# Strassen blocks for the first FFN's input products, float64 weights decoded by ACT's parametric ReLU, and split weights kept in DRAM, in a kernel of attention and two FFNs

## The chip, the cores and the metric

The kernel runs on one core of one Trainium2 chip. The metric is the device time of one execution in microseconds. Engines: PE multiplies matrices (PEld is its weight load), DVE works elementwise on vectors, ACT evaluates functions and copies, POOL is a third elementwise engine which here also can issue DMAs, and SP issues DMAs. SBUF is the on-chip memory, PSUM holds the eight banks that PE accumulates into.

## What is computed

```python
def reference(q, k, v, moe_w_gate, moe_w_val, moe_w_out, moe_rms_g, moe2_w_in, moe2_w_out):
    x = causal_attention(q, k, v)            # (2, 12, 448, 64) -> (896, 768), float32
    xn = x / sqrt(mean(x * x) + 1e-6) * moe_rms_g
    g = xn @ moe_w_gate                      # 768 -> 1536
    y = (g * sigmoid(g) * (xn @ moe_w_val)) @ moe_w_out          # 1536 -> 768
    h = y @ moe2_w_in                        # 768 -> 2048
    return maximum(0.01 * h, h) @ moe2_w_out                     # 2048 -> 768
```

All weights of the FFNs arrive as float64 (8 bytes a number, read on the chip as pairs of 32-bit words: `top` and, in the changed kernel, `low`).

## The kernel before

There are two batches of 448 tokens (b = 0, 1), 768 features in six blocks of 128, and feature-major tiles of 128 x 448. Each float32 operand is kept as a high and a low part of PE's fp32r type, and each product of two 128-blocks is three matmuls into one PSUM bank: high x high, high x low, low x high (lines 657 to 659, 879 to 881 and 1006 to 1008).

*Weights.* A float64 weight tile (128 x 768, 768 KB) is loaded by SP into one of two `raw` tiles, turned into float32 in `x` by one ACT scaling (line 308, or 263 in the second FFN) and three DVE instructions: a 16-bit copy (310, 265), a shift with a mask (312, 267) and a shift with an or (315, 270). Then it is split into high and low: ACT copies the high part (317, or 283 by halves), DVE subtracts for the low part (319, 284). `weight` does this for the first FFN into four `hl` tiles; `convert` and `split` do it by halves for the second.

*First FFN.* A column tile `fc` (12 of them, 128 columns each) of gate and value needs 6 blocks x 3 matmuls for each of g, v and each batch. `gate` issues these 18, `gate_out` applies silu, multiplies and splits the result into a `big` tile. Tiles 0 to 4 are done early for batch 0, beside the attention of batch 1; tiles 3 and 4 for batch 1 follow with the weights that are still there; tiles 5 to 11 are done for both batches; then the weights of tiles 0 to 2 are loaded, decoded and split a second time for batch 1. The output product runs over six column tiles `dc` with all 12 blocks in one go in two banks. When a `dc` is done, its y is split and four sums and differences of batch halves are formed and split (lines 809 to 828).

*Second FFN.* `pair` does two column tiles of the input product for both batches by one level of Strassen's method in Winograd's form: 2 x 2 blocks (columns by feature halves times feature halves by batches), seven block products of 3 x 3 matmuls in place of eight. Weight sums and differences are formed on DVE (888 to 923), banks are passed on by ACT copies (939, 943) and DVE additions (946, 949). `partial` multiplies a chunk of four results with the output weights and adds to partial sums in SBUF: ACT copies the partial sum into the bank (997) and back out (1015). The order is pair 0, pair 1, chunk 0, pair 2, pair 3, chunk 1, and so on.

*What sets the order.* Every step is registered with `add(engine, cost, ..., rank)`. `Order.emit` goes through the steps with those costs and fixes, for each engine, one static order: of the steps that are ready, the one of lowest rank goes first. A table `ADJUST` shifts single ranks of attention and early weights. On the chip each engine works through its own list strictly, waiting on semaphores; SP issues loads, the small transfers of the attention (`mrow`, `st`) and the outputs from one list.

Of the kernel before, what the change touches and what calls it, by code (L numbers as in the profile page):

```python
# [8 lines left out]
F32 = mybir.dt.float32  # L9
# [4 lines left out]
U16 = mybir.dt.uint16  # L14
# [8 lines left out]
    ("cut", 0): 19, ("cut", 1): 9, ("cut", 2): 7, ("cut", 3): 12, ("cut", 4): 43, ("cut", 6): 5,  # L23
    ("cut", 8): 21, ("cut", 10): 9, ("cut", 11): 18, ("exp", 0): 10, ("exp", 1): 59, ("exp", 2): 4,
    ("exp", 3): -11, ("exp", 4): -13, ("exp", 5): 39, ("exp", 7): 33, ("exp", 8): 83, ("exp", 9): 57,
    ("exp", 10): -21, ("g", 0, 0): -36, ("g", 2, 0): -51, ("g", 3, 0): -10, ("g", 4, 0): 49, ("gw", 0): -7,
    ("gw", 1): 35, ("gw", 2): 41, ("gw", 4): 11, ("gw", 5): 28, ("inv", 0): 253, ("inv", 1): 45,
    ("inv", 2): 28, ("inv", 3): -1, ("inv", 5): -49, ("inv", 8): -16, ("inv", 9): 30, ("inv", 10): -32,
    ("inv", 11): 54, ("max", 0): -4, ("max", 1): -68, ("max", 2): -70, ("max", 3): -16, ("max", 4): 14,
    ("max", 5): -17, ("max", 6): -33, ("max", 7): -38, ("max", 8): -5, ("max", 9): -8, ("max", 10): 36,  # L30
    ("max", 11): -2, ("mul", 1): 4, ("mul", 3): -23, ("mul", 5): -15, ("mul", 7): 9, ("mul", 9): -14,
    ("mul", 10): 21, ("round", 0): -22, ("round", 4): 42, ("round", 6): 51, ("round", 7): 11,
    ("round", 8): -50, ("round", 9): 119, ("round", 10): -8, ("row", 0): -43, ("row", 2): 6, ("row", 3): 24,
    ("row", 4): 5, ("row", 5): -100, ("row", 7): -18, ("row", 8): -6, ("row", 9): -13, ("row", 10): -178,
    ("sq", 0): -30, ("sq", 2): 3, ("sq", 3): -9, ("sq", 4): 34, ("sq", 5): -38, ("sq", 7): -22, ("sq", 8): -9,
    ("sq", 9): 8, ("sq", 11): -1, ("sum", 0): 49, ("sum", 1): 149, ("sum", 2): 1, ("sum", 3): 28,
    ("sum", 5): -19, ("sum", 6): 60, ("sum", 7): -70, ("sum", 8): -21, ("sum", 9): -51, ("sum", 10): 28,
    ("sum", 11): 10, ("turn", 0): -30, ("turn", 1): -8, ("turn", 2): 1, ("turn", 3): 8, ("turn", 5): 21,
    ("turn", 6): 46, ("turn", 7): -155, ("turn", 8): -9, ("turn", 9): -10, ("turn", 10): -44,
    ("turn", 11): 25, ("v", 1, 0): -14, ("v", 3, 0): -97, ("v", 4, 0): -96, ("val", 0): -90, ("val", 1): -183,  # L40
    ("val", 3): -120, ("val", 4): 50, ("val", 5): -22, ("val", 6): -21, ("val", 7): 3, ("val", 8): 13,
    ("val", 9): -43, ("val", 10): 17, ("val", 11): 13, ("vw", 0): -38, ("vw", 1): 189, ("vw", 3): -6,
    ("vw", 4): -94, ("vw", 5): -20,
}

# [98 lines left out]
def causal_attention_two_ffns(  # L144
# [61 lines left out]
    y = xn  # L206
# [3 lines left out]
    NT1 = B * KF  # L210
    NBIG = NT1 + 6
# [3 lines left out]
    tmps, parts = [], []  # L215
    tctx = ExitStack()
    order = [(fc, 0) for fc in range(EARLY)]
    order += [(fc, b) for fc in range(KF) for b in range(B) if (fc, b) not in order]
    t_slot = {k: n for n, k in enumerate(order)}
    NG = 12  # L220
    g_slot = {(fc, b): HK + (fc * B + b) % NG for fc in range(KF2) for b in range(B)}

    queue = []
    for fc in list(range(KF)) + list(range(EARLY - 2)):
        again = len(queue) >= 2 * KF
        queue += [(("g", fc, again), w_gate[fc]), (("v", fc, again), w_val[fc])]
    out_order = [dc for k in range(HK) for dc in (k, k + HK)]  # L230
# [11 lines left out]
    halves2 = [(hl, j) for hl in range(NHL) for j in range(2)]  # L242
    half_turn = [0]

    def convert(key, rank):

        n = slot[key]
        src = queue[n][1]
        raw, t = raws[n % NRAW], n % NX2
        kr, kx = ("raw", n % NRAW), [("x", t, 0), ("x", t, 1)]  # L250
        top = raw.bitcast(U32).rearrange("p (n t) -> p n t", t=2)[:, :, 1]
        halves = raw.bitcast(U16).rearrange("p (n t) -> p n t", t=4)
# [5 lines left out]
        def half(j):  # L258
            return lambda: xs32[t][:, j * HK * P:(j + 1) * HK * P]

        add("SP", 0.35, lambda: nc.sync.dma_start(out=raw, in_=src), r=[("split", n - NRAW)], w=[kr],
            rank=rank - 30, name=(key[0] + "d", key[1], 0), late=2.0, size=1024 * NW)
        add("ACT", 0.9, lambda: nc.scalar.activation(xs32[t], top.bitcast(F32), AF.Copy, scale=2.0 ** -112),  # L263
            r=[kr], w=kx + ([("x", t)] if t < NX else []), rank=rank, name=name)
        add("DVE", 0.56, lambda: nc.vector.tensor_copy(halves[:, :, 2], halves[:, :, 1]), port=True,  # L265
            w=[kr], rank=rank, name=name)
        add("DVE", 0.56, port=True, name=name, fn=lambda: nc.vector.tensor_scalar(
            top.bitcast(I32), top.bitcast(I32), 13, -0x7FFFFFF9, ALU.arith_shift_right, ALU.bitwise_and),
# [822 lines left out]
```

## Time and profile before

| what | value |
|---|---|
| time, median of 3 runs (lowest to highest) | 606.61 us (605.12 to 611.77) |
| profiled execution | 608.25 us |
| its span from first to last instruction | 606.5 us |
| PE busy | 590.6 us, 97% |
| DVE busy | 454.9 us, 75% |
| ACT busy | 319.3 us, 53% |
| DMA | 70.38 MB, mean 116 GB/s |
| chain of work that ended last | PE 85%, DVE 7%, DMA 3%, ACT 2%, issue 2% |

Matmuls overlap: one takes some 366 ns from its start to its end, but starts follow each other at about 0.2 us, so busy time merges overlapping matmuls, and the number that counts is the distance between starts. A view by stretches gives, for each stretch of time, the busy time of each engine with the number of instructions in brackets, the granted clock of PE as a share of full speed, and the DMA share.

### The profile page before, as it was taken

The numbers are of one execution on the slowest core, as the hardware profiler recorded it, in microseconds if no ns is written. First come the engines' busy times: TensorE is split into PE (matmuls) and PEld (weight loads), VectorE is DVE, ScalarE is ACT, GpSimd is POOL, SyncE is SP. The second block draws the span as 40 slices with busy tenths as digits, with TensorE's granted clock in tenths as the row PEclk, the third lists the DMA queues.
The fourth block names the chain that finished last, engine by engine and source line by source line (L and its number), as shares of the span: only waits on it lengthen the run. The fifth ranks groups of instructions, "written<-read, shape, count | busy, mean of one in ns | idle before, by whom it ended". The sixth has DMA issues, their size and how long they took to land.

```text
span 606.5 us, 8664 instructions
## 1 busy us (share of the span) xinstructions
PE 590.6 (97%) x3224; PEld 503.9 (83%) x3224; DVE 454.9 (75%) x844; ACT 319.3 (53%) x553; POOL 54.5 (9%) x84
## 2 busy tenths in 40 slices
PE   8989799999999999999999999899999999999997
PEld 6544456588999999999999999789999999999996
DVE  6678798789897666668778672997898879878920
ACT  3556675846444333344335331665587658746841
POOL 1246445430000000000000000000000000000000
PEclk8989899999999999999999999999999999999999
DMA  5283840443444333234444231205423342333122
GB/s 191 68 184 99 204 103 3 107 106 108 154 156 157 104 105 105 104 109 161 153 156 150 105 111 45 101 5 160 163 94 116 145 156 69 139 105 105 52 92 91
DMA packets 18714, 70.38 MB, mean 116 GB/s; under 512 B 6000, under 2 KB 7536, under 8 KB 18672
## 3 DMA queue, kind: packets, MB, share of 16 engines
q1 hardware_dynamic: 18672, 69.83, 36.5%
q8 instruction: 25, 0.41, 0.3%
q14 instruction: 17, 0.14, 0.1%
HBM read 66.85 MB, written 2.75 MB: 115 GB/s over the span
## 4 chain that ended last, share of the span: by engine, by line
PE 85%; DVE 7%; DMA 3%; ACT 2%; issue 2%; SPq 1%; POOL 0%; DVEq 0%; ACTq 0%
PE bank L657 13%; PE bank L659 13%; PE bank L658 13%; PE bank L1008 7%; PE bank L1007 7%; PE bank L1006 7%; PE bank L879 5%; PE bank L881 5%; PE bank L880 5%; PE bank L485 3%; PE bank L527 2%; PE bank L421 2%; PE bank L539 1%; DMA mrow<-mt 1%; PE bank L479 1%
## 5 line engine op out<-in xcount | busy, mean ns | idle before, releaser
L657 PE MATMUL bank<-xn,hl 128*128 128x448 f32 x288 | 106.7, 370 | 0.3 <-ACT sg L700 0.3
L659 PE MATMUL bank<-xn,hl 128*128 128x448 f32 x288 | 105.5, 366 | 0.1
L658 PE MATMUL bank<-xn,hl 128*128 128x448 f32 x288 | 105.2, 365 | 0.0
L1006 PE MATMUL bank<-big,hl 128*128 128x448 f32 x192 | 70.7, 368 | 0.0
L1007 PE MATMUL bank<-big,hl 128*128 128x448 f32 x192 | 70.7, 368 | 0.0
L1008 PE MATMUL bank<-big,hl 128*128 128x448 f32 x192 | 70.7, 368 | 0.0
L657 PEld LDWEIGHTS bank<-xn,hl 128*128 128x128 f32 x288 | 54.1, 188 | 7.1 <-issue 1.4
L319 DVE TENSOR_TENSOR hl<-x,hl 128x768 fp32r<-128x768 f32 x42 | 39.9, 955 | 25.0 <-ACT hl L317 24.7
L659 PEld LDWEIGHTS bank<-xn,hl 128*128 128x128 f32 x288 | 54.1, 188 | 5.4 <-DVE hl L319 1.1
L429 DVE CUSTOM_DVE_ANT_0 bank<-bank,maskw 112x224 f32<-112x224 f32 (+2 forms) x96 | 42.3, 469 | 20.6 <-PE bank L421 19.8
L658 PEld LDWEIGHTS bank<-xn,hl 128*128 128x128 f32 x288 | 54.1, 188 | 4.1
L317 ACT CAST hl<-x 128x768 fp32r<-128x768 f32 x42 | 34.9, 834 | 40.5 <-DVE x L315 22.9
L658 PE MATMUL bank<-big,hl 128*128 128x448 f32 x144 | 52.6, 365 | 0.0
L657 PE MATMUL bank<-big,hl 128*128 128x448 f32 x144 | 52.6, 365 | 0.0
L659 PE MATMUL bank<-big,hl 128*128 128x448 f32 x144 | 52.6, 365 | 0.0
L284 DVE TENSOR_TENSOR hl<-x,hl 128x384 fp32r<-128x384 f32 x72 | 38.8, 556 | 14.0 <-ACT hl L283 13.9
L310 DVE COPY raw<-raw 128x768 uint16<-128x768 uint16 x42 | 43.9, 1044 | 7.2 <-ACT x L308 7.0
L308 ACT ACTIVATE x<-raw 128x768 f32<-128x768 f32 x42 | 38.2, 909 | 9.2 <-DMA raw<-in_val 2.5
L283 ACT CAST hl<-x 128x384 fp32r<-128x384 f32 x72 | 35.6, 513 | 12.2 <-PE bank L880 4.1
L315 DVE SCALAR_TENSOR_TENSOR x<-x,raw 128x768 uint32<-128x768 uint32 x42 | 40.4, 962 | 0.8
L265 DVE COPY raw<-raw 128x768 uint16<-128x768 uint16 x32 | 33.4, 1043 | 9.6 <-ACT x L263 9.6
L1007 PEld LDWEIGHTS bank<-big,hl 128*128 128x128 f32 x192 | 36.0, 188 | 3.7
(120 smaller groups left out, 1162.8 us busy)
## 6 DMA issues: line engine op xcount, KB each, us to landing
raw<-in_out SPq DMA_DIRECT2D x28, 768.0 KB
raw<-in_in SPq DMA_DIRECT2D x16, 768.0 KB
raw<-in_gate SPq DMA_DIRECT2D x10, 768.0 KB
raw<-in_val SPq DMA_DIRECT2D x10, 768.0 KB
qkv<-in_qkv SPq DMA_DIRECT2D x32, 176.0 KB
raw<-in_gate SPq DMA_DIRECT2D x20, 192.0 KB
raw<-in_val SPq DMA_DIRECT2D x20, 192.0 KB
out<-sg SPq DMA_DIRECT2D x12, 224.0 KB
```

What stands on the lines that cost most here:

```text
L284: add("DVE", 0.5, port=True, name=name, fn=lambda: nc.vector.tensor_tensor(out=t[:, 1], in0=src(), in1=f32(t[:, 0]), op=ALU.subtract), r=[ ...
L308: add("ACT", 0.9, lambda: nc.scalar.activation(x[:, :w], top.bitcast(F32), AF.Copy, scale=2.0 ** -112), r=landed, w=[kx], rank=rank, name= ...
L310: add("DVE", 0.56, lambda: nc.vector.tensor_copy(halves[:, :, 2], halves[:, :, 1]), port=True, w=[kr], rank=rank, name=name)
L315: add("DVE", 0.96, port=True, name=name, fn=lambda: nc.vector.scalar_tensor_tensor(xb, xb, 3, top, ALU.logical_shift_left, ALU.bitwise_or) ...
L319: add("DVE", 0.96, port=True, name=name, fn=lambda: nc.vector.tensor_tensor(out=hl[:, 1, :w], in0=x[:, :w], in1=f32(hl[:, 0, :w]), op=ALU. ...
L429: nc.vector.tensor_tensor_reduce(out=s, in0=s, in1=maskw[:, S - w:S], scale=-1.0, scalar=3.0e38, op0=ALU.add, op1=ALU.min, accum_out=m[:, ...
L657: nc.tensor.matmul(o, hi, xh, start=s, stop=False, skip_group_check=True)
L658: nc.tensor.matmul(o, hi, xl, start=False, stop=False, skip_group_check=True)
L659: nc.tensor.matmul(o, lo, xh, start=False, stop=e, skip_group_check=True)
L1006: nc.tensor.matmul(bank(), hi, xh, start=s, stop=False, skip_group_check=True)
L1007: nc.tensor.matmul(bank(), hi, xl, start=False, stop=False, skip_group_check=True)
L1008: nc.tensor.matmul(bank(), lo, xh, start=False, stop=e, skip_group_check=True)
```

## The change

The changed kernel keeps the arithmetic of the parts but arranges the FFNs as follows.

- Tiles 5 to 11 of the first FFN (gate and value of one `fc` as the two columns) go through `pair`, as the second FFN's do. For this the two batch differences and sums of xn are formed once in `token_sums` from the float32 x, which is now kept in 12 tiles.
- The first FFN's output product is done in four chunks, over tiles (3, 4), (0, 1, 2), (5, 6, 7) and (8 to 11), with partial sums in the x tiles; `chunk` is one function for both FFNs.
- The float64 decoding is one ACT instruction with the parametric ReLU (slope 2^32 on the negative side) and two DVE instructions on the low word; the 16-bit copy is gone.
- The split weights of tiles 0 to 2 are stored to DRAM by SP (six stores of 768 KB) during the attention and reloaded by POOL's queue.
- Whole weight tiles are split at once into six wide tiles (and one half of each pair into two slim ones) in place of halves in four. The leaky ReLU is one ACT instruction. The sums of weights are formed in place.
- The second FFN's order is pairs 0, 1, 2, chunk 0, pairs 3, 4, chunk 1, and so on. Tiles are shared between stages, `ADJUST` has other numbers.

```diff
 ADJUST = {
-    ("cut", 0): 19, ("cut", 1): 9, ("cut", 2): 7, ("cut", 3): 12, ("cut", 4): 43, ("cut", 6): 5,
+    ("cut", 0): -30, ("cut", 1): -51, ("cut", 2): -5, ("cut", 3): 47, ("cut", 4): 7, ("cut", 5): -9,
...
+OUT1_CHUNKS = [3, 4], [0, 1, 2], [5, 6, 7], [8, 9, 10, 11]
+FIRST_FFN = [
+    ("n", 3), ("n", 4), ("n", 0), ("n", 1), ("c", 0), ("n", 2), ("s", 5), ("c", 1), ("s", 6), ("s", 7), ("s", 8),
+    ("c", 2), ("s", 9), ("s", 10), ("s", 11), ("c", 3),
+]
...
-        add("ACT", 0.9, lambda: nc.scalar.activation(xs32[t], top.bitcast(F32), AF.Copy, scale=2.0 ** -112),
...
-        add("DVE", 0.56, lambda: nc.vector.tensor_copy(halves[:, :, 2], halves[:, :, 1]), port=True,
...
+        add("ACT", 0.9, lambda: nc.scalar.activation(xs32[t], top.bitcast(F32), AF.Prelu, scale=2.0 ** -112,
+            alpha=2.0 ** 32),
...
         add("DVE", 0.56, port=True, name=name, fn=lambda: nc.vector.tensor_scalar(
-            top.bitcast(I32), top.bitcast(I32), 13, -0x7FFFFFF9, ALU.arith_shift_right, ALU.bitwise_and),
+            low, low, 29, None, ALU.logical_shift_right), w=[kl], rank=rank)
...
     def weight(key, rank, at=0.0):
+        hl, kh = hls[hl_of(key)], ("hl", hl_of(key))
+        if key in kept:
+            add("POOL", 1.3, lambda: nc.gpsimd.dma_start(out=hl, in_=stored[key[:2]]), r=[("kept", key[:2])], w=[kh],
+                rank=rank - 30, late=2.0, size=1024 * NW)
+            return
...
+        if (*key[:2], True) in kept:
+            add("SP", 0.35, lambda: nc.sync.dma_start(out=f32(stored[key[:2]]), in_=f32(hl)), r=[kh], w=[("kept", key[:2])],
+                rank=rank - 20, late=2.0, size=1024 * NW)
...
+    def pair(key1, key2, rank):
+        wr = rank - 2
+        a1, (a11, a12) = convert(key1, wr)
+        a2, (a21, a22) = convert(key2, wr)
+        A11, A12 = split(a1, wr)
+        A22, = split(a22, wr, False)
+        combine(a21, a11, a21, ALU.subtract, wr)
+        combine(a22, a22, a21, ALU.subtract, wr)
+        S3, S2 = split(a2, wr)
+        combine(a12, a12, a22, ALU.subtract, wr)
+        combine(a11, a22, a11, ALU.add, wr)
+        S1, S4 = split(a1, wr)
...
+    def gated(fc, rank):
+        (g0, kg0), (g1, kg1), (v0, kv0), (v1, kv1) = pair(("g", fc, False), ("v", fc, False), rank)
...
+    def token_sums(k, rank):
+        def both(b, dc, dst):
+            hi_lo(lambda: x32[b * KD + dc], x_key(b, dc), *dst, rank, ["room"])
+        minus((0, k), (1, k), (0, k), rank)
+        both(0, k, of_sum(0, k))
...
```

In the order of the instructions, three places matter. The first is PE's list in the first FFN: gate, then value of a column tile before (`hl_71`, `hl_70` the split weights, `bank_75`, `bank_76` the sums), and the first Strassen pair (tile 5) in the changed kernel.

```order
L658 MATMUL bank_75<-xn,hl_71 128x448
L659 MATMUL bank_75<-xn,hl_71 128x448
L657 MATMUL bank_76<-xn,hl_70 128x448
L658 MATMUL bank_76<-xn,hl_70 128x448
L659 MATMUL bank_76<-xn,hl_70 128x448
```

```order
L889 MATMUL bank_76<-xn,hl_68 128x448
L890 MATMUL bank_76<-xn,hl_68 128x448
L995 MATMUL bank_72<-big_93,hl_71 128x448
L996 MATMUL bank_72<-big_93,hl_71 128x448
L997 MATMUL bank_72<-big_93,hl_71 128x448
L888 MATMUL bank_79<-sum_1500,hl_70 128x448
L889 MATMUL bank_79<-sum_1500,hl_70 128x448
L890 MATMUL bank_79<-sum_1500,hl_70 128x448
L888 MATMUL bank_79<-sum_1501,hl_70 128x448
```

Blocks of nine matmuls on xn and on the token sums have taken the place of runs of 18, and a product of the next chunk (lines 995 to 997) stands between two blocks.

The second is DVE's list where weight tiles are decoded: two tiles of the first FFN's output weights before, and the weights of a pair (tile 6) in the changed kernel.

```order
L310 COPY raw_64<-raw_64 128x768
L312 TENSOR_SCALAR raw_64<-raw_64 128x768
L315 SCALAR_TENSOR_TENSOR x_66<-x_66,raw_64 128x768
L310 COPY raw_65<-raw_65 128x768
L312 TENSOR_SCALAR raw_65<-raw_65 128x768
L319 TENSOR_TENSOR hl_70<-x_66,hl_70 128x768
L315 SCALAR_TENSOR_TENSOR x_67<-x_67,raw_65 128x768
```

```order
L312 TENSOR_TENSOR more_1513<-x_67,more_1513 128x768
L295 SCALAR_TENSOR_TENSOR x_67<-x_67,raw_64 128x768
L897 TENSOR_TENSOR x_67<-x_66,x_67 128x384
L293 TENSOR_SCALAR raw_65<-raw_65 128x768
L295 SCALAR_TENSOR_TENSOR x_1518<-x_1518,raw_65 128x768
L312 TENSOR_TENSOR hl_68<-x_66,hl_68 128x768
L933 TENSOR_TENSOR sg_1517<-bank_77,sg_1516 128x448
```

Each tile has one instruction less for decoding; half-wide sums (line 897) and the pair's recombination (line 933) have come in between.

The third is SP's list in the middle of the attention (`qkv` are the attention's inputs, `mrow` the row maxima, `st` the row sums, `raw` the weights).

```order
L400 DMA qkv_96<-in_qkv 32x1408 x4
L465 DMA mrow_101<-mt_113 4x4x112
L556 DMA st_125<-sm_121 128x1x14 x2
L465 DMA mrow_102<-mt_114 4x4x112
L400 DMA qkv_93<-in_qkv 32x1408 x4
```

```order
L433 DMA qkv_111<-in_qkv 32x1408 x4
L498 DMA mrow_120<-mt_132 4x4x112
L354 DMA stored_g_105<-hl_68 128x1536
L589 DMA st_140<-sm_138 128x1x14 x2
L498 DMA mrow_121<-mt_133 4x4x112
L433 DMA qkv_112<-in_qkv 32x1408 x4
```

A store of 768 KB now stands ahead of small transfers that the attention waits for; there are six such stores in the list, and POOL's list has got six loads at its end.

## Rows read from the trace of the kernel before

**Rows 1.** Part 1 of the page: busy time, share of the span, instructions.
```profile
PE 590.6 (97%) x3224; PEld 503.9 (83%) x3224; DVE 454.9 (75%) x844; ACT 319.3 (53%) x553; POOL 54.5 (9%) x84
```
**Rows 2.** Stretches of 50 us: busy (count) of PE, PEld, DVE, ACT, POOL; clock; DMA.
```profile
0.00:50.00 50.00, 45.42 (x341) 28.23 (x342) 34.23 (x142) 24.31 (x39) 14.28 (x34) 0.90 0.53 148
50.00:100.00 50.00, 45.41 (x385) 26.41 (x379) 42.42 (x132) 32.78 (x59) 24.06 (x34) 0.97 0.47 110
...
150.00:200.00 50.00, 50.00 (x249) 46.33 (x248) 42.88 (x58) 23.11 (x34) 0.00 (x0) 1.00 0.43 144
...
350.00:400.00 50.00, 47.18 (x231) 42.49 (x229) 34.77 (x59) 22.00 (x43) 0.00 (x0) 1.00 0.24 79
400.00:450.00 50.00, 50.00 (x242) 45.44 (x243) 43.95 (x73) 29.60 (x57) 0.00 (x0) 1.00 0.37 126
```
**Rows 3.** PE alone in the two long stretches without idle time: busy (matmuls), clock.
```profile
143.30:379.65 236.35, 236.35 (x1167) 1.00 0.36 122
400.30:602.60 202.30, 202.30 (x980) 1.00 0.32 110
```
**Rows 4.** Timeline of PE from 380 to 400 us: start, us, instruction, idle before.
```profile
381.47 0.47 PE L879 MATMUL bank<-xn,hl 128*128 128x448 f32 x1 [1.44 <-ACT hl L283]
...
392.24 0.47 PE L879 MATMUL bank<-big,hl 128*128 128x448 f32 x1 [0.59 <-DVE sg L946]
...
399.98 0.47 PE L879 MATMUL bank<-xn,hl 128*128 128x448 f32 x1 [0.79 <-ACT bank L943]
```
**Rows 5.** Who PE waited for until 150 us: us in total, times, longest.
```profile
PE bank L479 <- DMA mrow<-mt: 2.8, 2, 1.8
PE bank L421 <- ACT qkr L411: 2.2, 2, 1.5
...
PE bank L421 <- DVE m L429: 1.0, 3, 0.6
PE bank L539 <- DVE mt L463: 0.8, 1, 0.8
PE bank L460 <- DVE mhl L458: 0.7, 2, 0.4
```
**Rows 6.** Groups of instructions by line and shape: count, busy us, mean ns, idle before.
```profile
L310 DVE COPY raw<-raw 128x768 uint16<-128x768 uint16 x42 | 43.9, 1044 | 7.2 <-ACT x L308 7.0
L315 DVE SCALAR_TENSOR_TENSOR x<-x,raw 128x768 uint32<-128x768 uint32 x42 | 40.4, 962 | 0.8
L319 DVE TENSOR_TENSOR hl<-x,hl 128x768 fp32r<-128x768 f32 x42 | 39.9, 955 | 25.0 <-ACT hl L317 24.7
L284 DVE TENSOR_TENSOR hl<-x,hl 128x384 fp32r<-128x384 f32 x72 | 38.8, 556 | 14.0 <-ACT hl L283 13.9
L308 ACT ACTIVATE x<-raw 128x768 f32<-128x768 f32 x42 | 38.2, 909 | 9.2 <-DMA raw<-in_val 2.5 <-DVE hl L319 2.4 <-DMA raw<-in_out 2.0
...
L312 DVE TENSOR_SCALAR raw<-raw 128x768 int32<-128x768 int32 x42 | 25.0, 596 | 1.2
...
L1015 ACT COPY part<-bank 128x448 f32<-128x448 f32 x36 | 19.1, 531 | 24.6 <-PE bank L1008 24.4
...
L946 DVE TENSOR_TENSOR sg<-bank,sg 128x448 f32<-128x448 f32 x8 | 5.0, 620 | 2.1 <-PE bank L881 2.1
...
L559 DVE SCALAR_TENSOR_TENSOR r<-st 128x14 f32<-128x14 f32 x12 | 4.0, 337 | 0.0
```
**Rows 7.** Timeline from 116 to 122 us, SP's queue, POOL and DVE.
```profile
116.77 2.52 SPq L301 DMA_DIRECT2D raw<-in_val  x4
...
118.52 1.44 POOL L582 TENSOR_TENSOR acc<-acc,sq 128x448 f32<-128x448 f32 x1 [0.74 <-ACT sq L579]
...
118.87 1.12 DVE L559 SCALAR_TENSOR_TENSOR r<-st 128x14 f32<-128x14 f32 x1
...
121.17 1.04 DVE L310 COPY raw<-raw 128x768 uint16<-128x768 uint16 x1
```
**Rows 8.** Engines in 10 us after a stall of PE: PE, PEld, DVE, ACT, POOL, clock.
```profile
60.00:70.00 10.00, 8.27 (x65) 4.55 (x65) 7.13 (x24) 5.42 (x10) 3.66 (x6) 0.83 0.90 197
```

More of the change, by code (lines that the diff above doesn't have):

```diff
@@ L33 @@
[L33 to L37, printed above, removed]
@@ L288, in weight, with split, t @@
-    def weight(key, rank, at=0.0):
-        n = slot[key]
-        src = queue[n][1]
+            xb(), xb(), 3, low, ALU.logical_shift_left, ALU.bitwise_or), r=[kl], w=kx + [("split", n)], rank=rank)
+        return (lambda: xs32[t], kx), [(half(j), [kx[j]]) for j in range(2)]
+    def split(part, rank, wide=True):
+        src, keys = part
+        turn, n = (wide_turn, NWIDE) if wide else (slim_turn, NSLIM)
+        m = turn[0] % n
+        turn[0] += 1
+        key = ("hl", m) if wide else ("slim", m)
+        def t(e):
+            return (slims[m] if not wide else hls[m] if m < NHL else more[m - NHL])[:, e]
+        add("ACT", 0.83 if wide else 0.51, lambda: nc.scalar.copy(t(0), src()),
+            r=keys if wide and m < NHL else keys + ["room"], w=[key], rank=rank)
+        add("DVE", 0.96 if wide else 0.56, port=True, fn=lambda: nc.vector.tensor_tensor(
+            out=t(1), in0=src(), in1=f32(t(0)), op=ALU.subtract), r=keys, w=[key], rank=rank)
+        return [(t, key, j) for j in range(2 if wide else 1)]
@@ L865, in of_y, with x_key @@
[L865 to L881 removed]
+    def x_key(b, k):
+        return ("x32", b * KD + k)
@@ new lines, in minus, with of_x, of_sum @@
+    def minus(o, p, q, rank):
+        (bo, ko), (bp, kp), (bq, kq) = o, p, q
+        o, p, q = (x32[b * KD + k] for b, k in (o, p, q))
+        add("DVE", 0.63, port=True, fn=lambda: nc.vector.tensor_tensor(out=o, in0=p, in1=q, op=ALU.subtract),
+            r=[x_key(bp, kp), x_key(bq, kq)], w=[x_key(bo, ko)], rank=rank)
+    def of_x(b, k):
+        return lambda e: xn[:, e, k, b * S:(b + 1) * S], ("xn", b, k)
+    def of_sum(n, k):
+        return lambda e: sums[n * HK + k][:, e], ("sum", n, k)
@@ new lines, in block @@
+    def block(u, weights, xs, first, rank, name):
+        t, wk, j = weights
+        def passes(k, x):
+            hi, lo = (t(e)[:, (j * HK + k) * P:(j * HK + k + 1) * P] for e in range(2))
+            o = banks[u][:, :S]
+            nc.tensor.matmul(o, hi, x(0), start=first and not k, stop=False, skip_group_check=True)
+            nc.tensor.matmul(o, hi, x(1), start=False, stop=False, skip_group_check=True)
+            nc.tensor.matmul(o, lo, x(0), start=False, stop=k == HK - 1, skip_group_check=True)
```

535 lines of the change are left out of this document (239 added, 296 removed).

## The prediction

> **What bounds the kernel now.** I read the page's first part, then the engines by stretches, then PE alone. PE is busy for 590.6 of 606.5 us, DVE for three quarters and ACT for half [rows 1]. By stretches the span has two regimes [rows 2]. From 0 to about 143 us (attention, with early first-FFN tiles beside it) PE has holes: 4.6 us in each of the first two stretches of 50 us. After that PE shows 50.00 of 50 us almost everywhere, and only the stretch at 350 us lacks 2.8 us, so nothing but PE's own work or that hole can be shortened there.
>
> How long that work takes is the distance between matmul starts, which the stretches of PE alone give [rows 3]. Between 143.30 and 379.65 us, 1,167 matmuls follow each other without a hole, which is 1,166 steps: 236.35 / 1,166 = 202.7 ns each. Between 400.30 and 602.60 us it is 202.30 / 979 = 206.6 ns, at the same granted clock of 1.00 and the same tile sizes. So there are two paces, 3.9 ns apart, and the pace changed at a restart, after PE had stood still at 399.98 us [rows 4]; it stayed to the end. The slower pace costs 979 x 3.9 ns = 3.8 us.
>
> The hole between 380 and 400 us is the passage from the first FFN to the second: PE waits 1.44 us for an ACT split of pair weights, 0.59 us for a DVE addition and 0.79 us for an ACT copy, 2.82 us in all [rows 4]. There DVE had to split y and its sums and decode the pair's weights at once.
>
> **The change part by part.** I sum against the profiled execution, 608.25 us (span 606.5 plus 1.75 around it); it lies 1.64 us above the median, 606.61.
>
> *Fewer matmuls.* A first-FFN tile for both batches is 2 x 2 x 6 products of three matmuls, 72. As a pair it is seven blocks of nine, 63. Seven tiles (5 to 11) change, so 7 x 9 = 63 matmuls go, all in the regime in which PE has no holes. At 202.7 ns that is 12.8 us (at 206.6 ns, 13.0). Tiles 0 to 4, the output products and the second FFN keep their counts. Value: -12.8 us.
>
> TensorE's rule would give less. The Trainium skill (TensorE: Matmul & The Clock Gate, Back-to-back issue gap) gives N/2.4 + 2.5 ns for an isolated stream, 189 ns at N = 448, so an estimate of 11.9 us for 63; the trace's 202.7 ns disagrees and is what I use.
>
> *The passage at 380 us.* Decoding a tile before costs DVE 1,044 + 596 + 962 ns, a whole split 955, a half split 556, a sum of 448 columns 620 [rows 6]. A pair before: 2 x 2.60 for decoding, seven half splits and four half sums at 0.556, ten instructions of 0.62 for the results: 17.5 us. A pair now: 2 x 1.56 (the 1,044 ns copy is gone; the shift works on as many words as the old one, so I take its 596 ns), three wide splits, one half split, four half sums, six instructions of 0.62: 3.1 + 2.9 + 2.8 + 3.7 = 12.5 us, against 63 x 0.2027 = 12.8 us of PE. The six wide tiles also let the first pair be ready before y is. So the causes of the 2.82 us shrink, but y's splits and sums still fall due within the last chunk. I take half: -1.4 us; ends -2.8 and 0.
>
> *New work late in the first FFN.* Tiles 9 to 11 and the last chunk take PE 333 x 0.2027 = 67.5 us. In that time DVE must prepare tiles 10 and 11 (2 x 8.8), finish three tiles (3 x 3.7), decode and split four output weights (4 x 2.51), form y's sums (33 x 0.62, of which the last 5 us fall behind the chunk) and prepare the first pair of the second FFN (8.8): about 63 us, 93%. The fullest stretch in which DVE before kept PE without holes is 43.95 of 50 us, 88% [rows 2]. If 88% is all that DVE can do, the 63 us need 71.1, 3.6 us too many; if it can do 93%, nothing is lost. I take +1.0; ends 0 and +3.6. ACT has room: it is busy 53% before [rows 1], and the chunks add 36 copies into and 36 out of banks at 0.53 us [rows 6], 38 us over the 213 us of PE in the first FFN.
>
> *The pace.* Some restarts in the trace lead to the quick pace, the last one to the slow. I can't tell which the changed kernel falls into; I take a little more of the quick one than before, -1.0; ends -3.8 (all quick) and +4.3 (the 1,103 quick ones that remain become slow).
>
> *Attention.* The decoding of ten early tiles loses its copy: 10 x 1.044 = 10.4 us of DVE in a regime where DVE is busy 42.4 of 50 us [rows 2]. PE waits there for DVE for 1.0 + 0.8 + 0.7 = 2.5 us, for `mrow` transfers 2.8 us and for ACT behind a `qkv` load 2.2 us [rows 5]. I take 1.5 us of the DVE waits as gained. The six stores (a tile of 768 KB each, in SP's list ahead of `mrow` and `st`) come on top of ten loads of the same size beside which those 2.8 us of `mrow` waits arose: 0.28 us a transfer, so +1.7 us for six. A stall costs more than itself: in the 10 us with the 1.5 us wait of PE the clock is 0.83 [rows 5, 8]. Sum +0.2; ends -4 (all DVE waits and part of the others go, with their clock) and +6 (1 us a store).
>
> *The reload.* Tile 0's gate weights go into `hl2` when batch 1 of tile 3 has done with them, and PE's list has 18 products, 54 matmuls or 10.9 us, before it wants them. A load of that size took at most 4.4 us from its issue to the first DVE instruction on it [rows 7]. So it is hidden with 6.5 us to spare, as for the others; six decodings and splits go from DVE and ACT, and PE sees nothing: 0. The ACT instruction with the parametric ReLU I take at the 909 ns of the scaling it replaces [rows 6]; it is on no path that PE waits for, and the list of ACT has four table loads before and after.
>
> Sum: -12.8 - 1.4 + 1.0 - 1.0 + 0.2 = -14.0, so 608.25 - 14.0 = 594.2 for an execution like the profiled one, and less 1.64, 592.6 for the median.
>
> **The rivals.**
>
> *DVE becomes the bound* (same within 1%). The first FFN's end at 88% costs 3.6 in place of 1.0, the holes at 380 us stay (0 in place of -1.4), and every restart falls into the slow pace (+4.3 in place of -1.0): 592.6 + 2.6 + 1.4 + 5.3 = 601.9 us. For it: 93% is more than any stretch before. Against: over the whole first FFN from 143 us DVE has about 175 us of work for 213 us of PE, and the second FFN falls from some 88% to 35.0 of 54.7 us for two pairs and a chunk.
>
> *The reload comes late* (about the same). In the trace a small DVE instruction (337 ns on average) took 1.12 us while POOL added two tiles [rows 6, 7]: the two engines hold each other up. If a reload issued by POOL were held up in the same ratio, three times a load, 13.2 us in place of 4.4, each of the first four would miss its 10.9 us by 2.3 us: +9.2, 601.8 us. Against: DVE is not busy without a break there, and the last two reloads have a chunk's time. The Trainium skill (SBUF — State Buffer, SBUF: two separate sides) speaks for this rival: a DMA from POOL's queue has its descriptors written by POOL, which two-port DVE instructions (shifts among them) lock out. No run so far has such a DMA; the skill's example is 0.62 us that became 3.1, which as an estimate adds 2.5 us and stays under the cover.
>
> *The stores choke the attention* (slower). Each of the six stores stands ahead of small transfers for which PE waits within microseconds. If each held PE back by its whole 4.4 us, that is 26.4 us in place of my 1.7: 617.3 us. It decides from (606.6 - 590.9) / 6 = 2.6 us a store. For it: PE did wait 1.8 us for one `mrow` [rows 5]. Against: ten transfers of the same size cost 2.8 us together.
>
> *It doesn't do what it says*: if the planner filled the Strassen blocks with other work, the count would stay. PE's list has 2,928 rows in place of 2,991, exactly 63 fewer, so I give this nothing.
>
> **How the numbers follow.** My forecast has 0.79, with its own range of 585 to 600; DVE as the bound 0.12; the late reload 0.05; the choking stores 0.04. A measurement of this kernel tells about 1% from no change, 600.5 to 612.7 us. Of the forecast nearly all (0.78) lies below 600.5, of the DVE rival 0.05 and of the reload 0.03 when they come in part: faster 0.86. The rest of these is 0.10 for the same, and the stores make 0.04 slower. The low end, 584, has all holes at 380 us gone, the quick pace throughout and half of the best end in the attention (592.6 - 1.4 - 1.0 - 2.8 - 2.1 = 585.3, a microsecond below for spread); the high end, 601, takes in most of the two middle rivals.
>
> **What would show it.** Right: 63 matmuls fewer at 202 to 207 ns; no hole of PE over 1 us between the attention's end and the last matmul; DVE some 70 us less busy in all; reloads landing before PE wants them. Wrong: PE waiting for DVE splits in tiles 9 to 11 or in the last chunk of the first FFN; PE waiting for `mrow` next to a store, with a clock of 0.8 in that slice; PE waiting for a DMA from DRAM near 150 us. The forecast fails if these add to more than about 8 us.

## The result and the profile after

The changed kernel takes 586.54 us, the median of four executions (595.38, 586.67, 586.10, 586.41), against 607.26 for the kernel before (605.12 to 611.77). The ratio is 0.965 with the interval 0.958 to 0.972: 3.5% faster. The forecast was 592.6, 584 to 601: the direction and the range held, and the number was 6 us too high. One thing is needed to read the times: they fall into two groups 9 us apart, near 586 and near 595; the ratio uses the first group, while the profile is of the execution of 595.38 us (span 593.7).

Busy time and instructions on the page, as [rows 1]:

```profile
PE 581.8 (98%) x3161; PEld 492.5 (83%) x3161; DVE 391.7 (66%) x760; ACT 374.5 (63%) x636; POOL 52.2 (9%) x90
```

63 matmuls are gone, DVE is 63.2 us less busy, ACT 55 us more. The stretches of 50 us, as [rows 2], then PE alone in one of 400 us, as [rows 3] (busy time with the count, clock, DMA):

```profile
0.00:50.00 50.00, 45.35 (x329) 27.61 (x331) 34.35 (x136) 24.09 (x39) 12.94 (x35) 0.90 0.52 141
50.00:100.00 50.00, 46.52 (x403) 26.66 (x399) 40.77 (x133) 33.48 (x61) 21.43 (x34) 0.97 0.61 164
150.00:200.00 50.00, 50.00 (x244) 45.41 (x243) 33.06 (x56) 25.81 (x46) 3.41 (x6) 1.00 0.51 174
350.00:400.00 50.00, 50.00 (x244) 45.41 (x243) 43.12 (x70) 35.77 (x61) 0.00 (x0) 1.00 0.29 98
400.00:450.00 50.00, 50.00 (x243) 45.42 (x242) 33.29 (x50) 31.86 (x52) 0.00 (x0) 1.00 0.40 139
```

```profile
150.00:550.00 400.00, 400.00 (x1937) 1.00 0.36 123
```

The hole at 350 us, 2.8 us before, is gone: the whole stretch is 50.00. But PE now starts 244 matmuls in 50 us where before it started 249 in the stretch at 150 us: 400 / 1,936 = 206.6 ns, the slower of the two paces of [rows 3], at the same clock of 1.00, and here from the attention's end to the last matmul. Behind 145 us PE waits for nothing. What it waited for before that, as [rows 5]:

```profile
PE bank L512 <- DMA mrow<-mt: 3.2, 4, 1.6
...
PE bank L454 <- ACT qkr L444: 1.1, 2, 0.8
PE bank L512 <- ACT p L541: 0.9, 2, 0.7
PE bank L454 <- DVE m L462: 0.6, 2, 0.4
PE bank L493 <- DVE mhl L491: 0.6, 2, 0.4
```

Decoding and splitting, as [rows 6], and the reloads (median us from issue to landing at the end):

```profile
L295 DVE SCALAR_TENSOR_TENSOR x<-x,raw 128x768 uint32<-128x768 uint32 x58 | 55.3, 956 | 26.8 <-ACT x L290 25.9
L312 DVE TENSOR_TENSOR hl<-x,hl 128x768 fp32r<-128x768 f32 x48 | 45.5, 955 | 39.8 <-ACT hl L310 39.7
...
L290 ACT ACTIVATE x<-raw 128x768 f32<-128x768 f32 x58 | 52.6, 910 | 1.6 <-DMA raw<-in_gate 0.9
...
L293 DVE TENSOR_SCALAR raw<-raw 128x768 uint32<-128x768 uint32 x58 | 32.2, 557 | 14.0 <-DMA raw<-in_out 10.0
```

```profile
hl<-stored_g POOLq DMA_DIRECT2D x3, 768.0 KB, 4.8
hl<-stored_v POOLq DMA_DIRECT2D x3, 768.0 KB, 4.6
```

The parametric ReLU takes 910 ns, the scaling that it replaced 909. The reloads take 4.8 and 4.6 us in the median and 6.7 at most, of a forecast cover of 10.9.

Where the time went, profile against profile, by the starts in the two traces. The attention's last restart of PE is at 141.58 us with 2,169 matmuls to come; before it was at 143.05 with 2,230, two fewer than 2,169 + 63. So the attention ends 1.47 - 0.4 = 1.1 us earlier. The 63 matmuls are 12.8 us. Behind its restart before took 459.56 us from the first start to the last, 7.8 more than 2,229 steps of 202.7 ns; 3.9 of that is the pace of 979 matmuls, so the three holes cost not 2.8 but 3.9 us with the longer steps around each restart. After takes 448.13 us, 8.7 more than at 202.7 ns, and has no hole: that is the slow pace alone. At the quick one it would gain 1.1 + 12.8 + 3.9 + 3.9 = 21.7 on the profiled execution's 608.25, which makes 586.6: the first group of times. The slow pace for all 2,169, 8.6 us, makes the second. The 586.6 is the measure for the experiments below.

Late in the first FFN, where the prediction saw DVE as nearly full, the 333 matmuls of tiles 9 to 11 and of the last chunk stand between 297.90 and 366.7 us (1,080 follow, all of the second FFN). Columns as above:

```profile
297.90:366.70 68.80, 68.80 (x334) 62.51 (x333) 52.62 (x84) 45.15 (x78) 0.00 (x0) 1.00 0.31 103
```

DVE is busy there for 52.6 us, 76%, and not for 63.

### The profile page after: what moved, and what is told of

Its sections match the earlier page's. It is cut to its first block, busy times and chain, and to the rows that moved or that the text cites. A ratio compares the mean times of both kernels' runs of the same rounds, so it can differ in the third digit from the quotient of the medians.

```text
span 593.7 us, 8477 instructions
## 1 busy us (share of the span) xinstructions
PE 581.8 (98%) x3161; PEld 492.5 (83%) x3161; DVE 391.7 (66%) x760; ACT 374.5 (63%) x636; POOL 52.2 (9%) x90
## 4 chain that ended last, share of the span: by engine, by line
PE 90%; DMA 5%; DVE 2%; SPq 1%; ACT 1%; issue 1%; ACTq 0%; DVEq 0%
PE bank L997 12%; PE bank L996 12%; PE bank L995 12%; PE bank L890 11%; PE bank L888 11%; PE bank L889 11%; PE bank L690 5%; PE bank L691 4%; PE bank L692 4%; PE bank L518 3%; PE bank L560 2%; DMA mrow<-mt 2%; PE bank L454 1%; PE bank L512 1%; DMA st<-sm 1%; DMA raw<-in_gate 1%
## 5 line engine op out<-in xcount | busy, mean ns | idle before, releaser
L295 DVE SCALAR_TENSOR_TENSOR x<-x,raw 128x768 uint32<-128x768 uint32 x58 | 55.3, 956 | 26.8 <-ACT x L290 25.9
L1006 ACT COPY x<-bank 128x448 f32<-128x448 f32 x72 | 38.3, 532 | 51.0 <-PE bank L997 50.8
L995 PE MATMUL bank<-big,hl 128*128 128x448 f32 x147 | 54.1, 368 | 0.0
L996 PE MATMUL bank<-big,hl 128*128 128x448 f32 x147 | 54.1, 368 | 0.0
L997 PE MATMUL bank<-big,hl 128*128 128x448 f32 x147 | 54.1, 368 | 0.0
L290 ACT ACTIVATE x<-raw 128x768 f32<-128x768 f32 x58 | 52.6, 910 | 1.6 <-DMA raw<-in_gate 0.9
L995 PE MATMUL bank<-big,more 128*128 128x448 f32 x135 | 49.7, 368 | 0.0
L996 PE MATMUL bank<-big,more 128*128 128x448 f32 x135 | 49.7, 368 | 0.0
L997 PE MATMUL bank<-big,more 128*128 128x448 f32 x135 | 49.7, 368 | 0.0
L690 PE MATMUL bank<-xn,hl 128*128 128x448 f32 x120 | 45.5, 379 | 0.0
L692 PE MATMUL bank<-xn,hl 128*128 128x448 f32 x120 | 44.1, 367 | 0.0
L691 PE MATMUL bank<-xn,hl 128*128 128x448 f32 x120 | 44.0, 367 | 0.0
L293 DVE TENSOR_SCALAR raw<-raw 128x768 uint32<-128x768 uint32 x58 | 32.2, 557 | 14.0 <-DMA raw<-in_out 10.0
L722 DVE TENSOR_TENSOR big<-sg,big 128x448 fp32r<-128x448 f32 x47 | 28.6, 621 | 18.8 <-ACT big L721 18.8
L888 PE MATMUL bank<-xn,hl 128*128 128x448 f32 x105 | 38.6, 368 | 0.0
L889 PE MATMUL bank<-xn,hl 128*128 128x448 f32 x105 | 38.6, 368 | 0.0
L890 PE MATMUL bank<-xn,hl 128*128 128x448 f32 x105 | 38.6, 368 | 0.0
L987 ACT COPY bank<-x 128x448 f32<-128x448 f32 x72 | 37.9, 536 | 1.2
L541 ACT ACTIVATE p<-bank 128x512 f32<-128x512 f32 x48 | 26.1, 596 | 17.3 <-PE bank L518 17.3
```

The source lines that it names most:

```text
L295: add("DVE", 0.96, port=True, name=name, fn=lambda: nc.vector.scalar_tensor_tensor(xb(), xb(), 3, low, ALU.logical_shift_left, ALU.bitwise ...
L690: nc.tensor.matmul(o, hi, xh, start=s, stop=False, skip_group_check=True)
L691: nc.tensor.matmul(o, hi, xl, start=False, stop=False, skip_group_check=True)
L692: nc.tensor.matmul(o, lo, xh, start=False, stop=e, skip_group_check=True)
L888: nc.tensor.matmul(o, hi, x(0), start=first and not k, stop=False, skip_group_check=True)
L889: nc.tensor.matmul(o, hi, x(1), start=False, stop=False, skip_group_check=True)
```

## Experiments

"Last restart" is the start of the first long run of PE behind the attention, read from PE's timeline; behind it 2,169 matmuls follow unless said. In seven profiles with the changed kernel's order in the attention it lies at 139.78 to 143.47 us, so some 2 us either way is that section's own spread.

**e1: the same kernel again.**

> The changed kernel once more, unaltered. Its first four times were 595.38 (the profiled one), 586.67, 586.10 and 586.41 us. Theory A, two paces: the last restart of TensorE in the attention fixes the distance between matmul starts for all 2,167 matmuls that follow; 206.7 ns gives 595.4, 202.7 ns gives 2,166 x 3.95 ns = 8.6 us less, 586.8. Then every time falls near 586.5 or near 595, none between, and a profiled run near 586.5 shows 202.7 ns a step (439 us from the last restart to the end in place of 447.7) at the same granted clock of 1.00. Rival B, a disturbance elsewhere: the quick runs have the same 206.7 ns a step and lose 9 us in the attention or at the edges of the span.

594.24, 585.22, 585.23, 595.23 us; nothing between. The profiled one is the first, and it again shows x1937 in the 400 us. So the groups are real: 5 of 8 executions near 586, 3 near 595. Theory A is borne out at the slow end; quick profiles come below.

**e2: the first FFN's tiles 5 to 11 without Strassen.** Here results of these tiles go into places that in this order still hold batch 1's input, so the values are not the reference's; number and shape of the instructions are.

```diff
-    ..., ("s", 5), ("c", 1), ("s", 6), ("s", 7), ("s", 8), ("c", 2), ("s", 9), ("s", 10), ("s", 11), ("c", 3),
+    ..., ("n", 5), ("c", 1), ("n", 6), ("n", 7), ("n", 8), ("c", 2), ("n", 9), ("n", 10), ("n", 11), ("c", 3),
```

> Tiles 5 to 11 of the first FFN as whole products again, without Strassen; chunks, decoding, stored weights and shared tiles stay. Theory A, the gain is first of all the 63 matmuls: 63 more, all behind the attention and without a hole, 63 x 202.7 ns = 12.8 us (13.0 at 206.7 ns), so about 599.5 us at the quick pace and 608.5 at the slow one. Rival B, the gain came from the passage, the decoding and the attention, and Strassen only shifts load to DVE: 63 matmuls more cost 5 us or less (592 or lower) because holes that Strassen makes are gone; there are none in the trace, so I expect A.

600.45 us (599.51 to 601.01). The profile is quick from its last restart (141.57) to the end but for one hole, PE's line in the timeline:

```profile
390.49 0.47 PE L888 MATMUL bank<-xn,hl 128*128 128x448 f32 x1 [0.61 <-ACT bank L926]
```

Against 586.6 that is 13.8: 63 x 202.7 ns = 12.8, and 1.0 for the hole, its restart and one longer step at 404.59 us. Theory A; the matmuls are the largest term and cost what the distance of starts says.

**e3: the old decoding in the changed kernel.** ACT scales, DVE copies 16 bits, masks and ors; the planner makes its own order.

```diff
-    ... AF.Prelu, scale=2.0 ** -112, alpha=2.0 ** 32)
+    ... AF.Copy, scale=2.0 ** -112)
+    add("DVE", 0.56, lambda: nc.vector.tensor_copy(halves[:, :, 2], halves[:, :, 1]), ...
```

> The changed kernel with the decoding of the kernel before: a scaling on ACT in place of the parametric ReLU, and one more DVE copy of 16-bit halves for each weight tile (about 1.04 us each). Theory A, DVE's load was what held PE up: late in the first FFN DVE then has about 73 us of work for 67.5 us of PE, so holes of 5 us or more come back between 200 and 400 us, and 1 to 1.5 us in the attention: about 593 us at the quick pace, more if a restart falls into the slow one. Rival B, the order of chunks and the shared tiles removed the holes, and DVE has slack for the copy: no hole over 1 us after the attention, 1 to 1.5 us more in the attention, about 588 us at the quick pace.

595.81 us (592.48 to 598.26). The last restart comes at 148.65, with 18 matmuls fewer to come: 3.4 us later than after. Behind it one stretch (columns as above), and PE's one named wait, from the timeline:

```profile
350.00:400.00 50.00, 49.39 (x240) 44.59 (x239) 46.34 (x74) 33.90 (x60) 0.00 (x0) 1.00 0.19 65
```

```profile
397.03 0.47 PE L893 MATMUL bank<-sum,hl 128*128 128x448 f32 x1 [0.61 <-ACT bank L931]
```

DVE is busy 93% of that stretch and PE loses 0.6 us, to an ACT copy. Of the 7.5 us by which the profiled execution (594.11) lies above 586.6, 3.4 are the attention's, 0.9 this hole with its restart, 0.5 two steps that no wait is named for, and 2.6 a slow pace of 646 steps between 262 and 396 us. Neither theory: the attention pays more than either said, the first FFN far less than A.

**e4: the kernel before with the new decoding alone.**

```diff
-    ... AF.Copy, scale=2.0 ** -112)
+    ... AF.Prelu, scale=2.0 ** -112, alpha=2.0 ** 32)
-    add("DVE", 0.56, lambda: nc.vector.tensor_copy(halves[:, :, 2], halves[:, :, 1]), ...
```

> The kernel before with the new decoding alone (parametric ReLU on ACT, no 16-bit copy on DVE); nothing else changes. Theory A, DVE's load made the holes: of the 2.82 us at the passage from the first FFN to the second under 1 us is left, the attention ends about 1.5 us earlier, and with fewer restarts the pace may stay quick to the end (-3.9): 607.3 - 3.3 = 604.0 us, or 600 at the quick pace throughout. Rival B, the order of the passage (y's splits, sums and the first pair in one place) made them: the 2.8 us stay, only the attention gains: about 605.8 us.

616.52 us (611.12 to 622.10), ratio 1.009 (1.004 to 1.014) to the kernel before beside it. With one instruction less per tile the planner chose another order for the attention; 2,232 matmuls are left at 152.15, some 9.5 us later than before, and the profiled execution (622.10) is slow from there to the end. So this tells little of decoding, but it does tell of the passage, by the stretch and the timeline:

```profile
350.00:400.00 50.00, 48.63 (x235) 43.66 (x234) 24.38 (x42) 16.20 (x29) 0.00 (x0) 1.00 0.19 64
```

```profile
396.97 0.47 PE L877 MATMUL bank<-xn,hl 128*128 128x448 f32 x1 [1.36 <-ACT hl L282]
```

DVE is busy for half of the stretch, and the first hole of [rows 4] is still there. Right before it DVE is busier, after ten microseconds with 1.18 us of work:

```profile
391.00:396.90 5.90, 4.61 (x23) 3.84 (x21) 4.38 (x8) 3.58 (x7) 0.00 (x0) 1.00 0.00 0
```

These eight instructions split y, its sums and a half of the pair's weights; no decoding starts behind 377 us. So decoding doesn't make this hole. By the lists the hole comes of the splits and sums that fall due at once; these were not tried apart.

**e5: the same with the order kept.** The planner still counts the copy, which no longer issues anything.

```diff
-        add("DVE", 0.56, lambda: nc.vector.tensor_copy(halves[:, :, 2], halves[:, :, 1]), port=True,
+        add("DVE", 0.56, lambda: None, port=True,
```

> The kernel before with the new decoding, and this time the planner still counts the 16-bit copy that no longer stands there, so that every engine's list keeps the order of before, less 75 DVE copies. In the first attempt the planner's order changed too, and the attention became 9 us longer. Theory A, DVE's load made the attention's waits: the attention ends 1.5 us or more before the 143 us of before; the hole at the passage near 380 us was made by the chain from the last bank through y and its sums, which has no decoding in it, so it stays at 2 to 3 us: 607 - 1.5 to -3 = 604 to 606 us at the pace mix of before. Rival B: DVE's load made that hole too, it falls under 1 us: 602 to 604 us. Rival C: DVE has slack everywhere, nothing moves: 607.

602.96 us over ten (600.40 to 608.36), ratio 0.988 (0.984 to 0.992) to the kernel before beside it. In the profile (603.66 us) the attention is not earlier: 2,241 matmuls are left at 142.09, before 2,230 at 143.05, so it is 1.3 us later. Of the three holes only the first stands, and all 2,241 matmuls are quick:

```profile
382.71 0.47 PE L881 MATMUL bank<-xn,hl 128*128 128x448 f32 x1 [1.43 <-ACT hl L284]
```

So DVE's relief closed the second and the third hole (0.59 and 0.79 us) and with them two chances of a slow pace; A holds for the first hole, B for the others. In the attention no gain shows; with a spread of 2 us and one profile a small one is not excluded.

**e6: one DVE copy more per decoding, order kept.**

```diff
+            nc.vector.tensor_copy(half16, half16)
             nc.vector.tensor_scalar(low, low, 29, None, ALU.logical_shift_right)
```

> The changed kernel with its order unaltered and one DVE copy more in front of each decoding (a 16-bit half onto itself, the form of the removed copy, about 1.04 us each, 68 of them, 71 us of DVE). Prediction's theory: late in the first FFN DVE has 63 us of work for 67.5 us of PE, and 11 us more do not fit, so PE waits there for 4 us or more, and the attention gets 1.5 us longer: 592 or more at the quick pace (585.2 to 586.7 without the copy). Rival: DVE has slack behind the attention because the weights' wide tiles and the planner spread the work, no hole over 0.5 us there, and only the ten early decodings in the attention cost 1 to 3 us: 587 to 589 at the quick pace, 596 to 598 at the slow one.

597.81 us (597.25 to 598.95), 11 us more than the quick group. The last restart is at 147.81: 6.2 us for ten copies in the attention. Behind it PE takes 4.4 us more than 2,168 steps of 202.7 ns; its named waits there (us in total, times, longest), and three stretches:

```profile
PE bank L899 <- DVE sg L944: 1.4, 1, 1.4
PE bank L1007 <- DVE big L733: 0.6, 1, 0.6
```

```profile
350.00:400.00 50.00, 49.88 (x245) 45.56 (x244) 47.79 (x77) 35.22 (x61) 0.00 (x0) 1.00 0.24 79
400.00:450.00 50.00, 48.61 (x241) 44.71 (x240) 42.11 (x58) 30.78 (x51) 0.00 (x0) 1.00 0.45 150
```

```profile
388.00:408.40 20.40, 19.01 (x92) 16.59 (x90) 19.22 (x28) 14.05 (x23) 0.00 (x0) 1.00 0.38 122
```

Where DVE is busiest by stretches of 50 us, 47.79, PE loses 0.12 us, and the 1.4 us come in one where it is busy 42.11. But the wait, at 408.5 us, ends 20 us in which DVE is busy 94%: the pair's result `sg` stands in its list behind decodings. So a full DVE does make PE wait, and only just behind the stretch that looks fullest. The other 2.4 of the 4.4 us lie in restarts and steps that no wait is named for. The time is the one of the prediction's theory, but more than half of the excess is the attention's.

**e7: each store twice, order kept.**

```diff
     nc.sync.dma_start(out=f32(stored[key[:2]]), in_=f32(hl))
+    nc.sync.dma_start(out=f32(again[key[:2]]), in_=f32(hl))
```

> The changed kernel with each of the six stores of split weights issued twice (the second into a place of its own in DRAM that nothing reads), order otherwise unaltered. If a store costs the 0.28 us that the prediction took, six more add 1.7 us to the end of the attention (141.6 us in the first profile); if stores choke the small transfers at 2.6 us or more each, 16 us or more; if they run beside everything, under 0.5 us. I expect under 1 us: 585 to 587 at the quick pace, 594 to 596 at the slow one.

595.07 us (593.09 to 596.37). The profile is quick throughout, so none of this is the pace: the last restart is at 151.10, 9.5 us later. PE's waits until 160 us:

```profile
PE bank L516 <- DMA mrow<-mt: 5.2, 3, 3.5
PE bank L458 <- ACT qkr L448: 2.8, 2, 2.6
PE bank L696 <- DVE hl L350: 2.8, 1, 2.8
```

Six more stores cost 1.6 us each: `mrow` behind them, and a weight tile that came late. I expected under 1 us for all six; the rival that stores choke small transfers is real, for stores that the order doesn't have a place for.

**e9: stores and reloads cut to a twelfth.** The reload is cut in the same way as the store, so that most of the weights of tiles 0 to 2 are not those of the reference.

```diff
-    nc.sync.dma_start(out=f32(stored[key[:2]]), in_=f32(hl))
+    nc.sync.dma_start(out=f32(stored[key[:2]])[:, :, :64], in_=f32(hl)[:, :, :64])
```

> The changed kernel, its order unaltered, with the six stores and the six reloads cut to 64 of 768 columns of each part; the rest of tiles 0 to 2 keeps what lay in the buffers, so the output is not the reference's. The doubled stores made the attention end 9.5 us later (its last restart at 151.1 us in place of 141.6), 1.6 us a store. Theory A, the six stores that are there cost as much each: the last restart falls near 132 us and the time by 9 us, 577 at the quick pace. Rival B, the order was made with these six in it and their transfers lie beside other waits; only what is added to that order collides: the last restart stays within 1.5 us of 140 to 141.6 us, 584 to 587 at the quick pace, 593 to 596 at the slow one.

585.27 us (584.90 to 587.69), last restart at 139.78: B. That is 1.8 us before the profile after and 0.6 before e1, inside the spread. So the six stores that are there don't cost 1.6 us each; the 0.28 us that the prediction took can't be told from nothing.

**e10: the old table.** All of `ADJUST` from the kernel before.

```diff
-    ("cut", 0): -30, ("cut", 1): -51, ("cut", 2): -5, ("cut", 3): 47, ("cut", 4): 7, ("cut", 5): -9,
+    ("cut", 0): 19, ("cut", 1): 9, ("cut", 2): 7, ("cut", 3): 12, ("cut", 4): 43, ("cut", 6): 5,
```

> The changed kernel with the planner's table of corrections from the kernel before; nothing else changes, so the attention's order is another. Theory A, the attention lives from its table, and the 1.5 us that it gained are the table's as much as DVE's: with the old table it ends 3 to 9 us later, as with every other change to its order or load so far (+6 with the extra copies, +9.5 with the doubled stores, +9 with the planner's own order for the kernel before): 589 to 596 at the quick pace. Rival B, DVE's relief made the gain and the table does nothing: last restart within 1.5 us of 140 to 141.6, 585 to 588 at the quick pace, 594 to 597 at the slow one. In either case no hole over 1 us behind the attention.

599.82 us (597.88 to 609.25). The last restart is at 152.98, 11.4 us later; PE's waits up to 160 us and, from the timeline behind the restart, a reload that PE waited for:

```profile
PE bank L511 <- DMA mrow<-mt: 4.4, 3, 2.0
PE bank L453 <- DVE m L461: 3.7, 4, 1.4
PE bank L559 <- ACT x L601: 2.3, 1, 2.3
```

```profile
189.20 0.48 PE L689 MATMUL bank<-xn,hl 128*128 128x448 f32 x1 [0.64 <-DMA hl<-stored_g]
```

Theory A, beyond its 9 us. The changed kernel's attention lives from the table made for it.

**e8: restarts on purpose.** A small matmul after every 24 products of the chunks and pairs. It begins a sum of its own in spare columns of a bank that products may be using, and the output isn't the reference's.

```diff
+        if made[0] % 24 == 0:
+            c = (64, 48, 32, 16, 8)[made[0] // 24 % 5]
+            nc.tensor.matmul(SM[:, S:S + c], w, x[:, :c], start=True, stop=True, skip_group_check=True)
```

> The changed kernel with a small matmul (64, 48, 32, 16 or 8 columns in turn, into columns of a bank that nothing else uses) after every 72 matmuls of the chunks and pairs behind the attention, 27 in all. Theory A, each irregular step in the stream decides anew between the two paces: the profile shows stretches of 71 steps at 202.7 and others at 206.7 ns, and the times lie between 586 and 595 us plus about 27 x 0.1 = 2.7 us, close together. Rival B, the pace belongs to the whole execution (set once, by something outside the stream): all stretches have one pace, and the times still fall into two groups 8 to 9 us apart.

592.49 us (590.94 to 593.25), no groups: theory A. PE's timeline around one of 64 columns, and around one of 48 a stretch later:

```profile
331.51 0.37 PE L897 MATMUL bank<-xn,hl 128*128 128x448 f32 x1
331.72 0.37 PE L898 MATMUL bank<-xn,hl 128*128 128x448 f32 x1
331.93 0.19 PE L887 MATMUL bank<-xn,hl 128*128 128x64 f32 x1
331.95 0.44 PE L896 MATMUL bank<-sum,slim 128*128 128x448 f32 x1
332.24 0.36 PE L897 MATMUL bank<-sum,slim 128*128 128x448 f32 x1
332.43 0.36 PE L898 MATMUL bank<-sum,slim 128*128 128x448 f32 x1
...
346.42 0.36 PE L1006 MATMUL bank<-big,more 128*128 128x448 f32 x1
346.62 0.18 PE L887 MATMUL bank<-big,more 128*128 128x48 f32 x1
346.65 0.45 PE L1004 MATMUL bank<-big,more 128*128 128x448 f32 x1
346.94 0.37 PE L1005 MATMUL bank<-big,more 128*128 128x448 f32 x1
347.15 0.37 PE L1006 MATMUL bank<-big,more 128*128 128x448 f32 x1
```

Ahead of the first the starts lie 0.21 us apart, behind it (0.29 for the restart) 0.19, 0.20 and on at 202.7 ns; behind the second 0.21 again. Of the 27, ten stood in a slow stretch, and the quick pace followed all ten (the expectation of e11 below says twelve, a miscount). Of the 17 in a quick one, 11 were followed by the slow pace; the five of 64 columns, three in quick and two in slow stretches, all by the quick one.

The starts to the nanosecond tell more. The quick pace repeats four steps of about 203, 202, 199 and 207 ns, the slow one three of 207, 207 and 206. All 11 that led from the quick pace to the slow one stood behind two steps of 202 or 203 ns. Three of 48 columns, after which the pace stayed quick, stood behind a step of 199 or 200 ns, as did one of 32 in e11. The three of 64 columns stood where the 11 did, and the pace stayed quick. So in these two runs the outcome follows, every time, from the place in the rhythm and the width; the counts are a few cases that repeat.

**e11: four small matmuls, and then none.** 32, 16, 8 and 64 columns after 24, 48, 72 and 96 products behind the attention; these only add (`start=False`) to columns that nothing reads.

```diff
+    widths = {24: 32, 48: 16, 72: 8, 96: 64}
+        if c := widths.get(made[0]):
+            nc.tensor.matmul(SM[:, S:S + c], w, x[:, :c], start=False, stop=False, skip_group_check=True)
```

> The changed kernel with four small matmuls (32, 16, 8 and 64 columns, adding to columns of a bank that nothing reads), one after each 72 of the first 288 matmuls behind the attention. In the earlier run such a matmul in a stretch of the slow pace was followed by the quick one 12 times in 12, and one of 64 columns by the quick pace 5 times in 5. Theory A, the pace is the phase in which the stream of weight loads and matmuls restarts: behind the fourth the stream is quick to the end, so all times fall between 585.5 and 589 us (585.2 to 586.7 with the quick pace from the start, 0.1 us for each small matmul, up to 288 x 4 ns = 1.2 us for a slow start), none near 595. Rival B, what follows a small matmul depends on more than that: half of the times stay near 594 to 596.

586.75 us (585.46 to 589.38), none near 595. The profile has a quick stretch behind the first, a slow one behind the second, a quick one behind the third, and the quick one behind the fourth to the end; the second's stretch and one of 340 us:

```profile
181.00:195.00 14.00, 14.00 (x70) 1.00 0.75 277
215.00:555.00 340.00, 340.00 (x1679) 1.00 0.33 114
```

340 / 1,678 = 202.6 ns. The profiled execution is the one of 589.38, and its excess is in the attention (last restart at 143.47). Four times of four would also come by luck at 5 in 8 each (15%); the trace is the stronger evidence. In its four executions this version has the time of the changed kernel's first group without the second.

**e12: four wide tiles in place of six.**

```diff
-    NWIDE = NHL + 2
+    NWIDE = NHL
```

> The changed kernel with four wide tiles for split weights in place of six, shared by chunks and pairs alike. With the new decoding alone the kernel before kept the first hole of its passage (1.43 us, PE waits for an ACT split of pair weights), the other two went. Theory A, the two extra tiles let the pair's weights be ready before the chunk in front of it has done with its own: with four, holes of 1 to 3 us stand behind each of the chunks that a pair follows (seven such places), 4 us or more in all behind the attention: 590 or more at the quick pace. Rival B, the planner finds another order and the holes stay away because DVE has less to do: under 1 us in all, 585 to 588 at the quick pace.

590.09 us (585.60 to 595.64). Behind the attention one hole, nine matmuls into the second pair of the second FFN:

```profile
377.46 0.47 PE L888 MATMUL bank<-sum,hl 128*128 128x448 f32 x1 [0.61 <-ACT bank L926]
```

It costs 1.0 us with its restart, and in the profile the 1,006 steps behind it are slow, 4.0 us more. Theory A is wrong by its seven places. In this profile the two more tiles are worth one small hole, and with it a chance of a slow restart.

## Why the prediction was right, and where its sizes were off

The main term and the direction were right by their mechanism. The terms sum to -14.0 in the forecast and to -21.7 by the profiles at the quick pace; every term that missed was too pessimistic, so no errors cancelled. Both groups of times lie inside 584 to 601, so that the range held says little of any single term.

*Fewer matmuls, -12.8.* Right, with its unit: 63 by the distance between starts (e2). The estimate of 189 ns, 11.9 us, from the formula of the Trainium skill (TensorE: Matmul & The Clock Gate, Back-to-back issue gap) is met by neither pace.

*The passage, -1.4.* Mis-sized: -2.8 of waiting, -3.9 with the restarts. Only half of the reason holds: the lighter decoding closed the second and third hole (e5), not the first (e4, e5). Fewer wide tiles did not bring the first back (e12); whether the chunks' order or the sums' place keeps it away was not tried apart.

*New work late in the first FFN, +1.0.* Nothing was lost. Two steps failed. The 63 us of DVE work were not all due in that time: DVE was busy 52.6 of 68.8 us there, 76%; three of y's sums with their splits, for one, follow behind it. And the 88% of [rows 2] is no ceiling: at 93% (e3) PE lost 0.6 us, to ACT and not to DVE. Near 96% DVE does cost PE something, 1.4 us at once (e6), and with DVE busy for half of a stretch PE can still wait 1.36 us (e4): the share over 50 us says little, what is due just before the wait says more. There is a slip as well: 63 us at 88% need 71.6 us, so the end of the term is +4.1 and not +3.6.

*The pace, -1.0.* Both ends of the bound were about right, -3.8 and +4.3 against -3.9 and +4.7, and none of the eight executions takes the value between. A choice between two states has two forecasts; I had one. This is the largest miss of the median, 2.9 us.

*Attention, +0.2.* The profile has -1.1 there, which lies inside the section's spread of 2 us, so neither a gain nor its cause is shown. The 1.5 us for the removed copies did not show in the old order (e5), though ten copies more cost 6.2 us in the new one (e6); the 1.7 us for the stores can't be told from nothing (e9). What the text left out is `ADJUST`: with the old table the new attention ends 11 us later (e10).

*The reload, 0.* Right: PE never waited for one, though the slowest took 6.7 us and not 4.4. The rule of the Trainium skill (SBUF — State Buffer, SBUF: two separate sides) named with that rival showed no harm here; the late reload (0.64 us, e10) came in another order.

Of the rivals, *DVE becomes the bound* is refuted by the full stretches; with 66 us more of DVE's work (391.7 to 457.8 us busy, e6) the time rises by 11. *The stores choke the attention* names a true mechanism with a price of 1.6 us for a store added to the order (e7), which those in it avoid (e9).

## What to carry to other kernels

A removed matmul on a stream without holes is worth the distance between starts, and that distance has to be read in each stretch, since it can have two values. Where an order was tuned with its transfers and instructions in it, what one of them costs can't be read from adding another; take it out or thin it, with the order kept, and treat a changed planner table as an edit of its own. A hole costs its wait, its restart and a chance of a slower pace behind it.

## What the runs showed that I had not expected

This stream of weight loads and 448-column matmuls has two steady rhythms at the same clock of 1.00: 206.7 and 202.7 ns a matmul. It keeps one through hundreds of microseconds (2,167 steps in e1 or e9), and an irregular step, a wait or a matmul of a few columns, can set the other. Behind a small matmul its width and its place in the quick rhythm told the outcome (e8, e11); behind a wait what decides is open. A 64-column matmul gave the quick pace each of the six times it was tried, at a cost of 0.1 us.
